# Loading one weight unevenly: six rows on every partition, eighteen more on twelve of them, forty on others

## The chip, the cores and the metric

The kernel runs on one core of a Trainium2 chip. The metric is the device time of one execution in microseconds (us). Its profile spans about 1.8 us less, from the first to the last instruction. KB is 1,024 bytes here, MB in the page 10^6 bytes; the prediction's rate of 27.1 KB/us counts 1,000 bytes to the KB.

## The reference, cut to what matters

Two branches on one token of width 1024 for a batch of two are mixed by a gate.

```python
def _A_ref(x, k_cache, v_cache, wq, wo):          # attention over a cache of 16384 positions, 32 heads
    q = ...(x @ wq)
    scores = einsum("bhqd,bhkd->bhqk", q, k_cache) * Dh ** -0.5
    o = einsum("bhqk,bhkd->bhqd", softmax(scores), v_cache)
    return ... o @ wo
def _B_ref(x, w1, w2, w3, w4):
    h = _gelu(_layernorm(x) @ w1)
    ...                                           # h is shifted by one or two positions
    hs = concatenate([g0, g1, g2, g3], axis=-1) @ w2
    x1 = x + hs
    return x1 + _gelu(_layernorm(x1) @ w3) @ w4
return g * a + (1 - g) * b
```

The two caches are 64 loads of 8 MB, about 94% of the 572.5 MB that are read. With one position every shift moves in zeros, so the input of `w2` is zero and `hs` is zero. The kernel loads and multiplies `w2` all the same. It also means that an experiment may leave rows of `w2` out without a wrong result (where one does, I say so), and that a correct result does not test the product of `w2` in any version.

## The kernel before

Everything large goes through three buffers of 64 KB per partition (8 MB each). One loop issues the loads in a fixed order as buffers come free: wq, K0, K1, V0, K2, V1, and so on. After V4, w1 and w2 share one buffer. At the end come w4 and wo in pieces.

```python
NBIG = 3
def big_tile(name):
    return big.tile([P, SLOT], BF16, tag="big", name=name)      # SLOT = 32768 elements
def load_k(i):
    t = big_tile("Kn")
    nc.sync.dma_start(out=t[:].rearrange("p (j d) -> p j d", d=Dh), in_=cache_rows(A_k_cache, i))
def load_rows(keys, srcs):
    t = big_tile("wt")
    c0 = 0
    for key, src in zip(keys, srcs):
        R, N = src.shape[0] // P, src.shape[1]
        v = t[:, c0 : c0 + R * N].rearrange("p (r n) -> p r n", n=N)
        nc.sync.dma_start(out=v, in_=src.rearrange("(p r) n -> p r n", p=P))
        wt[key] = v
        c0 += R * N
...
def linear(key, actT):                                           # w2 and w3: weights are the stationary side
    for c in range(C):
        for r in range(R):
            nc.tensor.matmul(ps[:, c, :], lhsT=w[:, r, :]...[:, :, c], rhs=actT[:, r, :], ...)
def st_mix():
    layernorm(xT[:], xn1T[:])
    ...                                                          # w1: activations stationary, 512 columns of w1 move
    nc.vector.tensor_tensor(out=x1[:], in0=xT[:], in1=linear("w2", shT)[:], op=ALU.add)
    layernorm(x1[:], xn2T[:])
    start_out(x1[:])
...
extra = {NT // 8: (lambda: load_rows(["w1", "w2"], [B_w1, B_w2]), st_mix), ...}
```

## Time and profile before

| quantity | before | where it is read |
|---|---|---|
| time | 1335.28 us (1335.23 to 1335.68) | three runs |
| share of 16 DMA engines' span, main queue | 99.4% | page, queue table |
| TensorE / VectorE busy | 61% / 57% | page, busy times |
| one 64 KB packet on one engine | 2.42 us | trace, packet records |
| queue ahead of the next V load at its issue | 19.2 us | timeline: 305.74 - 286.56 |

The page of the kernel before. The first lines are busy time and share of the span by engine; the DMA and GB/s lines have one figure for each of 40 slices; the queue lines are packets, MB and the time of their packets as a share of 16 engines.

```profile
span 1333.4 us, 11500 instructions
...
PE 811.7 (61%) x5017; PEld 353.2 (26%) x5017; DVE 758.8 (57%) x998; ACT 27.2 (2%) x68; POOL 13.2 (1%) x40
...
DMA  9999999999999999999999999999999999999997
GB/s 409 439 437 423 433 437 431 435 431 435 434 432 437 424 434 439 439 433 423 437 432 438 439 425 439 423 441 433 429 435 435 441 421 435 433 438 437 422 425 330
...
q1 hardware_dynamic: 12664, 572.54, 99.4%
q8 instruction: 39, 0.64, 0.2%
```

The DMA engines are busy throughout and the other engines are not. A load of K or V is 128 packets of 64 KB, eight on each of the 16 engines. At 2.42 us a packet an engine moves 26.5 KB per us.

The timeline of the kernel before around the layer that uses w2: start, duration, engine, line, operation, count, and the idle time with what ended it. SPq lines are DMA issues.

```profile
249.17 3.58 PE L559 MATMUL misc<-wt,xn1T 128*2 128x512 bf16 x16 [0.70 <-DVE xn1T L507]
...
252.68 4.01 PE L534 MATMUL misc<-shT,wt 128*128 128x2 bf16 x64
...
256.73 0.33 SPq L108 DMA_DIRECT2D Kn<-in_A_k_cache_dram  x1
...
265.88 2.37 DVE L339 STREAM_TRANSPOSE T<-Kn 128x1024 f32<-128x1024 f32 x2 [4.71 <-DMA Kn<-in_A_k_cache_dram]
...
286.56 0.33 SPq L119 DMA_DIRECT2D Vn<-in_A_v_cache_dram  x1
...
305.74 2.37 DVE L339 STREAM_TRANSPOSE T<-Kn 128x1024 f32<-128x1024 f32 x2 [8.08 <-DMA Kn<-in_A_k_cache_dram]
```

K7 is issued at 256.73 and its first transpose starts at 305.74, when it has landed. V6 is issued at 286.56, with that K7 still under way: 19 us of work are queued. The engines have something to do whenever a buffer is late by less than that.

The end of the chain of waits before, in order of time: start, duration, what.

```profile
1241.67 41.61 DMA Vn<-in_A_v_cache_dram
...
1292.98 26.76 DMA wo<-in_A_wo_dram
...
1319.76 9.92 DMA wo<-in_A_wo_dram
...
1330.16 0.42 DVE T L638
```

The chain ends in waits for the loads. Every 1 us by which the last wo piece lands later is 1 us of time.

One more reading is needed, and the views don't print it. The trace keeps the moment at which each of the 16 engines posts its completion of a transfer. Here are these moments for the kernel before, sorted, in us after the first of the 16:

```
V5 (second tile after w2)   0.0 0.2 0.3 0.3 0.4 0.4 0.7   1.5 1.6 1.6 1.7 1.7 1.7 1.7 1.9 1.9
last piece of wo            0.0 0.2 0.2 0.4 0.5 0.8 0.9   5.8 6.8 7.0 7.1 7.1 7.1 7.1 7.2 7.2
```

Seven engines are early and nine are late, and the gap grows. The late nine set the end.

### The profile page before, as it was taken

The page shows a single profiled execution, that of the slowest core. Times are in us where ns is not written, and L with a number is a line of the kernel's source. Part 1 is how long each engine was busy: PE and PEld are TensorE (multiplying, and loading weights), DVE is VectorE, ACT ScalarE, POOL GpSimd, SP SyncE. Part 2 cuts the span into 40 slices and gives each one's busy share as a digit, 9 for nine tenths or more (in the row PEclk, how much of TensorE's full clock was granted, in tenths as well). Part 3 has the DMA queues.
Part 4 walks back from the last instruction along what each step waited for, and adds up shares of the span by engine and source line. Part 5 has one row for each costly group of instructions (what it writes and reads, how often), then busy time and mean ns, then how long its engine had stood idle before and what let it go on. Part 6 is the DMA issues. An engine that isn't in the chain of part 4 may idle for free.

```text
span 1333.4 us, 11500 instructions
## 1 busy us (share of the span) xinstructions
PE 811.7 (61%) x5017; PEld 353.2 (26%) x5017; DVE 758.8 (57%) x998; ACT 27.2 (2%) x68; POOL 13.2 (1%) x40
## 2 busy tenths in 40 slices
PE   2577655676556765556766555576655556665564
PEld 0233222322225222222322222222222222222232
DVE  1677665466652665555666555566655556665540
ACT  0000000000000000000000000000000000000000
POOL 0000000000000000000000000000000000000000
PEclk9788877788777877778887777888777788877775
DMA  9999999999999999999999999999999999999997
GB/s 409 439 437 423 433 437 431 435 431 435 434 432 437 424 434 439 439 433 423 437 432 438 439 425 439 423 441 433 429 435 435 441 421 435 433 438 437 422 425 330
DMA packets 12722, 573.27 MB, mean 430 GB/s; under 512 B 1784, under 2 KB 1792, under 8 KB 2560
## 3 DMA queue, kind: packets, MB, share of 16 engines
q1 hardware_dynamic: 12664, 572.54, 99.4%
q8 instruction: 39, 0.64, 0.2%
q14 instruction: 11, 0.09, 0.0%
q10 hardware_dynamic: 8, 0.00, 0.0%
HBM read 572.53 MB, written 0.00 MB: 429 GB/s over the span
## 4 chain that ended last, share of the span: by engine, by line
PE 32%; DVE 29%; DMA 23%; another core or an unknown queue 12%; issue 2%; ACT 1%; SPq 0%; ACTq 0%; POOL 0%
DVE T L339 22%; PE S L353 21%; DMA Kn<-in_A_k_cache_dram 13%; PE O L397 7%; DMA wt<-in_B_w_dram 4%; DMA Vn<-in_A_v_cache_dram 3%; DMA wo<-in_A_wo_dram 3%; PE misc L224 2%; DVE Os L412 2%; PE misc L534 1%; ACT Pr L381 1%; DVE PT L385 1%; DVE mx L374 1%; PE misc L420 1%
## 5 line engine op out<-in xcount | busy, mean ns | idle before, releaser
L353 PE MATMUL S<-T,z 128*128 128x512 bf16 x2048 | 597.4, 425 | 316.4 <-DVE T L339 301.7
L339 DVE STREAM_TRANSPOSE T<-Kn 128x1024 f32<-128x1024 f32 x512 | 612.2, 1229 | 258.8 <-DMA Kn<-in_A_k_cache_dram 205.6
L353 PEld LDWEIGHTS <-z 128*128 128x128 bf16 x2048 | 211.0, 104 | 689.5 <-issue 528.0
L397 PE MATMUL O<-Vn,PT 128*32 128x512 bf16 x2048 | 121.4, 390 | 3.3 <-DMA Vn<-in_A_v_cache_dram 3.3
L397 PEld LDWEIGHTS <-PT 128*32 128x32 bf16 x2048 | 74.8, 141 | 48.7 <-issue 20.4
L408 DVE TENSOR_SCALAR Os<-O,xmask 128x128 f32<-128x128 f32 x32 | 11.2, 351 | 101.3 <-PE O L397 101.3
L224 PE MATMUL misc<-rs,ones_f 128*128 128x2 f32 x64 | 17.9, 349 | 79.1 <-DVE rs L428 79.1
L381 ACT ACTIVATE Pr<-S,nb 128x512 bf16<-128x512 f32 x32 | 22.0, 687 | 1196.8 <-DVE nb L376 1159.1
L420 PE MATMUL misc<-asel,Os 128*128 128x2 f32 x64 | 12.4, 264 | 51.0 <-DVE Os L412 51.0
L364 DVE TENSOR_REDUCE m<-S 128x1 f32<-128x512 f32 x32 | 22.1, 692 | 36.9 <-PE S L353 36.9
L385 DVE STREAM_TRANSPOSE PT<-Pr 128x512 bf16<-128x512 bf16 x32 | 22.8, 711 | 28.7 <-ACT Pr L381 28.7
L224 PEld LDWEIGHTS misc<-rs,ones_f 128*128 128x128 f32 x64 | 16.1, 313 | 84.0 <-issue 81.2
L412 DVE SCALAR_TENSOR_TENSOR Os<-O,xmask,Os 128x128 f32<-128x128 f32 x96 | 33.7, 351 | 3.4
L420 PEld LDWEIGHTS misc<-asel,Os 128*128 128x128 f32 x64 | 9.7, 191 | 65.2 <-DVE Os L412 61.0
L224 PE MATMUL misc<-mdiag,ones_f 128*128 128x128 f32 x64 | 15.5, 325 | 17.1 <-DVE mdiag L367 17.1
L374 DVE TENSOR_REDUCE mx<-misc 64x1 f32<-64x64 f32 x64 | 14.2, 222 | 19.1 <-PE misc L224 18.7
L313 POOL TENSOR_TENSOR z<-qsel,own 128x32 bf16<-128x32 bf16 x32 | 10.8, 336 | 1205.5 <-PE S L353 1175.1
L534 PEld LDWEIGHTS <-wt 128*128 128x128 bf16 x288 | 18.2, 164 | 8.4 <-DMA wt<-in_B_w_dram 7.6
L534 PE MATMUL misc<-xn2T,wt 128*128 128x2 bf16 x224 | 14.4, 202 | 7.4 <-DMA wt<-in_B_w_dram 7.4
L432 DVE RECIPROCAL rinv<-misc 128x2 f32<-128x2 f32 x32 | 5.4, 170 | 22.4 <-PE misc L224 22.4
L281 PE MATMUL misc<-wt,xT 128*2 128x512 bf16 x64 | 6.1, 562 | 19.9 <-DVE xT L269 19.9
L638 DVE CAST T<-out_acc 128x256 bf16<-128x256 f32 x1 | 0.4, 425 | 29.5 <-PE out_acc L446 29.5
(83 smaller groups left out, 109.0 us busy)
## 6 DMA issues: line engine op xcount, KB each, us to landing
Vn<-in_A_v_cache_dram SPq DMA_DIRECT2D x2, 4096.0 KB, 46.3
wt<-in_B_w_dram SPq DMA_DIRECT2D x1, 7168.0 KB
w<-in_B_w_dram SPq DMA_DIRECT2D x4, 1792.0 KB, 31.5
wo<-in_A_wo_dram SPq DMA_DIRECT2D x6, 1024.0 KB, 33.2
wt<-in_B_w_dram SPq DMA_DIRECT2D x2, 2048.0 KB, 37.1
wo<-in_A_wo_dram SPq DMA_DIRECT2D x2, 512.0 KB, 18.7
wo<-in_A_wo_dram SPq DMA_DIRECT2D x4, 256.0 KB, 12.7
Kn<-in_A_k_cache_dram SPq DMA_DIRECT2D x32, 51.7
```

Of the source, the lines that this page charges most:

```text
L224: nc.tensor.matmul(ps[:], lhsT=ones_f[:], rhs=src, start=True, stop=True)
L339: moved = nc.vector.transpose(out=T[:].rearrange("p w j s -> p j w s"), in_=Kw[:, m * CW : (m + 1) * CW].rearrange("p (j w e) -> p j w e", ...
L353: nc.tensor.matmul(S[:], lhsT=z[:, v, NM - 1 - m : NM - 1 - m + P], rhs=Tb[:, v // 2, :, v % 2], start=(m == 0 and v == 0), stop=(m == NM ...
L364: nc.vector.reduce_max(out=m[:], in_=S[:], axis=AX.X)
L374: nc.vector.reduce_max(out=mx[pa, :], in_=mall[pa, pa], axis=AX.X)
L381: nc.scalar.activation(out=Pr[:], in_=S[:], func=ACTF.Exp, bias=nb[:], scale=scale, accum_out=rs[:])
L385: nc.vector.transpose(out=PT[:], in_=Pr[:])
L397: nc.tensor.matmul(O[32 * g : 32 * g + 32, :], lhsT=PT[:, m : CJ * 32 : 16], rhs=V[:, j0 : j0 + 4, :], start=(m == 0), stop=(m == NM - 1),)
L408: nc.vector.tensor_scalar(out=Os[:], in0=Ox, scalar1=xmask[:, 0:1], scalar2=None, op0=ALU.mult)
L412: nc.vector.scalar_tensor_tensor(out=Os[:], in0=Ox, scalar=xmask[:, x : x + 1], in1=Os[:], op0=ALU.mult, op1=ALU.add,)
L420: nc.tensor.matmul(oc[:], lhsT=Os[:], rhs=asel[:], start=True, stop=True)
L534: nc.tensor.matmul(ps[:, c, :], lhsT=w[:, r, :].rearrange("k (p c) -> k p c", c=C)[:, :, c], rhs=actT[:, r, :], start=(r == 0), stop=(r == ...
```

## The change

Its intent, as I read it: put fewer bytes of w2 on most engines and more on a few, by placing 18 extra rows on each of partitions 0 to 11 through a transfer whose outermost dimension is three. The product has to follow the uneven layout: it now has the activations as the stationary side and adds up 25 row slots, some of them on few partitions, then transposes the result with 16 small matmuls.

```diff
+    WAYS, QUAD, BASE, MORE = 3, 4, 6, 18
+    W2_MORE = slice(0, WAYS * QUAD)
+    n_more = WAYS * QUAD * MORE
+    n_rest = D - P * BASE - n_more                     # 40
+    W2_REST = slice(64, 64 + n_rest)
+    W2_ROWS = (
+        [(slice(0, P), r) for r in range(BASE)]
+        + [(W2_MORE, BASE + r) for r in range(MORE)]
+        + [(W2_REST, BASE)]
+    )
... (an assert; load_rows returns its buffer; shT gets 24 row slots)
+    def load_w1_w2():
+        t = load_rows(["w1"], [B_w1])
+        w2 = t[:, KC * D : (KC + BASE + MORE) * D].rearrange("p (r n) -> p r n", n=D)
+        nc.sync.dma_start(
+            out=w2[:, 0:BASE, :], in_=B_w2[0 : P * BASE, :].rearrange("(p r) n -> p r n", p=P)
+        )
+        r0 = P * BASE
+        nc.sync.dma_start(
+            out=w2[W2_MORE, BASE : BASE + MORE, :],
+            in_=B_w2[r0 : r0 + n_more, :].rearrange("(y x r) n -> x y (r n)", x=WAYS, y=QUAD),
+        )
+        r0 += n_more
+        nc.sync.dma_start(out=w2[W2_REST, BASE, :], in_=B_w2[r0:D, :])
+        wt["w2"] = w2
... (half_rows: the product of w1 made into a helper with a list of row slots)
-        nc.vector.tensor_tensor(out=x1[:], in0=xT[:], in1=linear("w2", shT)[:], op=ALU.add)
+        hs = half_rows("w2", shT, W2_ROWS)
+        hs_ps = misc_psum([P, KC, B])
+        for c in range(KC):
+            for g in range(2):
+                nc.tensor.matmul(hs_ps[64 * g : 64 * g + 64, c, :],
+                    lhsT=hs[32 * g : 32 * g + 32, c : HW : KC],
+                    rhs=ident_f[32 * g : 32 * g + 32, group(g)], start=True, stop=True)
+        nc.vector.tensor_tensor(out=x1[:], in0=xT[:], in1=hs_ps[:], op=ALU.add)
...
-        NT // 8: (lambda: load_rows(["w1", "w2"], [B_w1, B_w2]), st_mix),
+        NT // 8: (load_w1_w2, st_mix),
```

More of the change, by code (lines that the diff above doesn't have):

```diff
@@ L121, in load_v @@
         vn_tiles[i] = t
+    WAYS, QUAD, BASE, MORE = 3, 4, 6, 18
+    W2_MORE = slice(0, WAYS * QUAD)
+    n_more = WAYS * QUAD * MORE
+    n_rest = D - P * BASE - n_more
+    assert 0 < n_rest <= 64 and KC + BASE + MORE <= SLOT // D
+    W2_REST = slice(64, 64 + n_rest)
[18 more added lines that the diff above has]
+        wt["w2"] = w2
     def load_rows(keys, srcs):
@@ L132, in load_rows @@
             c0 += R * N
+        return t
     W4_SPLIT = [7] * 4
@@ L525, in gelu, with half_rows @@
         nc.vector.tensor_tensor(out=dst_bf, in0=sq[:], in1=pre_f32, op=ALU.mult)
+    HW = D // 2
+    def half_rows(key, actT, slots):
+        w = wt.pop(key)
+        ps = misc_psum([P, HW])
+        for g in range(2):
+            zero_rows(ps, g, HW)
+        for n, (rows, r) in enumerate(slots):
+            for g in range(2):
+                nc.tensor.matmul(
+                    ps[group(g), :],
+                    lhsT=actT[rows, r, :],
+                    rhs=w[rows, r, g * HW : (g + 1) * HW],
+                    start=False,
+                    stop=(n == len(slots) - 1),
+                    skip_group_check=True,
+                )
+        out = t_tile([P, HW], FP32)
+        nc.vector.tensor_copy(out=out[0:64, :], in_=ps[0:64, :])
+        return out
     def linear(key, actT):
@@ L544 @@
     h_rows = const.tile([P, D // 2], BF16)
-    shT = const.tile([P, KC, B], BF16)
+    shT = const.tile([P, BASE + MORE, B], BF16)
     x1 = const.tile([P, KC, B], FP32)
@@ L551, in st_mix @@
         layernorm(xT[:], xn1T[:])
-        w1 = wt.pop("w1")
-        HW = D // 2
-        ps = misc_psum([P, HW])
-        for g in range(2):
-            zero_rows(ps, g, HW)
-        for r in range(KC):
-            for g in range(2):
-                nc.tensor.matmul(
-                    ps[group(g), :],
-                    lhsT=xn1T[:, r, :],
-                    rhs=w1[:, r, g * HW : (g + 1) * HW],
-                    start=False,
-                    stop=(r == KC - 1),
-                    skip_group_check=True,
-                )
-        h1 = t_tile([P, HW], FP32)
-        nc.vector.tensor_copy(out=h1[0:64, :], in_=ps[0:64, :])
+        h1 = half_rows("w1", xn1T, [(slice(0, P), r) for r in range(KC)])
         gelu(h1[0:64, :], h_rows[0:64, :])
@@ L574, in st_mix @@
                     raise NotImplementedError("one position only")
-        nc.vector.tensor_tensor(out=x1[:], in0=xT[:], in1=linear("w2", shT)[:], op=ALU.add)
+        hs = half_rows("w2", shT, W2_ROWS)
+        hs_ps = misc_psum([P, KC, B])
+        for c in range(KC):
+            for g in range(2):
+                nc.tensor.matmul(
+                    hs_ps[64 * g : 64 * g + 64, c, :],
+                    lhsT=hs[32 * g : 32 * g + 32, c : HW : KC],
+                    rhs=ident_f[32 * g : 32 * g + 32, group(g)],
+                    start=True,
+                    stop=True,
+                )
+        nc.vector.tensor_tensor(out=x1[:], in0=xT[:], in1=hs_ps[:], op=ALU.add)
         layernorm(x1[:], xn2T[:])
```

## The prediction

> **What bounds the kernel now.** The DMA engines. The page's slice table shows DMA at 9 tenths in every slice but the last, the queue table gives the main queue 99.4% of 16 engines' span, and the windows view shows a DMA share of 0.97 to 1.02 in every 33 us until the tail. PE (61%) and DVE (57%) have room. Each K or V tile is 8 MB, 128 packets of 64 KB, and the trace has 2.42 us for one such packet on one engine: 27.1 KB/us per engine. The queue is never empty: at most issues one whole tile (about 19.5 us) is still ahead.
>
> **Engines do not finish together.** The trace records when each of the 16 engines posts its completion of a transfer. For K0 these lie within 1.8 us; for the last wo piece within 7.2 us: 7 engines finish within 0.9 us of the first, 9 come 5.8 to 7.2 us later. [...]a fetch puts about 0.93 us between two data packets and makes the next one 0.5 us longer. The slow nine set the end of the kernel.
>
> **What the change does to DMA.** Bytes stay the same. [...] The loads of six rows stay at k = 16. [...]432 KB go to three engines, 144 KB each (four packets of 36 KB, an estimated 1.36 us each). The forty rows get k = 10, 8 KB each. Per engine, w2 costs 128 KB now[...]. That is +120 KB, +4.5 us on three engines, and -0.9 to -1.2 us on the others. A lag is not recovered while the queue stays full.
>
> **What it does to compute.** The 64 small matmuls of w2 (4.0 us in the timeline at 252.7) become 50 of 512 columns; the 16 of w1 took 3.58 us[...], so an estimated 11 us, some 8 us of it after the late rows land, plus 16 small transposing matmuls and a 0.7 us copy. The layer and the release of the slot move by 8 to 10 us, and K6's QK starts about 8 us late. The next K load was issued at 256.7 and landed 49 us later, so some 29 us of queue stood before it: no DMA bubble. DVE idled 8 us before K7, so compute catches up. Nothing of this is on the critical path.
>
> **Sum.** If at least one of the three engines is among the slow nine (I think 7 in 10), the end moves by about +4 to +4.5 us. If all three are among the fast seven, the lag disappears in their 6 us of slack, and the end moves by about -1 us. Prediction 1338.9 us, 8 in 10 between 1334.0 and 1341.5. Chances: faster 0.01, within 2% 0.97, slower 0.02.
>
> **What would show it.** Twelve packets of 36 KB on three engines; three late completions by about 4.5 us from K6 on, kept to the end; QK of K6 late, K7 not; matmul group of w2 about 10 us; DMA share 1.00 in the windows after it.
>
> **What would make it wrong.** A different k; a packet to few partitions slower than 27 KB/us; the later slot release emptying the queue; a fetch pattern that moves to other engines.

k is the number of engines that share a transfer; the trace after has three and ten completions where the prediction has three engines and k = 10. A fetch is one of the 39 packets of 16 KB on queue 8 (instruction). The sum came to +4 to +4.5 us if one of the three engines is late and about -1 us if all are early, put as 1338.9 us. Of the terms behind it the bytes by engine, by the completions after, are 120 KB more on three engines (4.5 us at 27.1 KB/us) and 24 or 32 KB less on the others (0.9 and 1.2 us).

## The result

The time after is 1335.02 us (1334.81 to 1335.45, six runs), before 1335.39 us (1335.23 to 1335.68, six runs of the kernel before): 0.37 us less by the medians. The ratio is 0.9997, with a 95% interval of 0.9984 to 1.001. Ratios are the mean time of one kernel's runs over that of the other's of the same rounds, so not quite the ratio of the medians quoted. All outputs are right. The verdict is: the same.

The page after:

```profile
span 1333.6 us, 11483 instructions
...
PE 797.4 (60%) x4974; PEld 351.3 (26%) x5037; DVE 760.1 (57%) x999; ACT 27.2 (2%) x68; POOL 12.8 (1%) x40
...
DMA  9999999999999999999999999999999999999998
GB/s 410 437 439 417 439 431 437 423 433 433 438 432 435 429 427 439 439 437 427 429 437 431 439 431 439 429 431 437 429 435 433 439 431 429 435 432 437 429 422 338
...
q1 hardware_dynamic: 12729, 572.54, 99.4%
q8 instruction: 39, 0.64, 0.2%
```

Nothing moves in these averages. The trace has what the sum hides. The DMA issues after, for w2 (KB each, and us to landing where a single wait shows it):

```profile
wt<-in_B_w_dram SPq DMA_DIRECT2D x1, 1536.0 KB, 41.4
...
wt<-in_B_w_dram SPq DMA_DIRECT2D x1, 432.0 KB
wt<-in_B_w_dram SPq DMA_DIRECT2D x1, 80.0 KB
```

The packet records show 128 packets of 12 KB, twelve of 36 KB that run three at a time, from 243.4 to 249.4 us of the span, and 40 of 2 KB. The trace has three completions for the load of 432 KB and ten for that of 80 KB. So the eighteen rows did go to three engines, four packets each, and the forty rows to ten. The last three of those ten completions, at 250.39 to 250.50 us, come after the three of the 432 KB, at 249.75 to 249.89, and the other seven by 246.72: the three engines are, by this, among the ten. The completions after, beside those of before:

```
V5      before   0.0 0.2 0.3 0.3 0.4 0.4 0.7   1.5 1.6 1.6 1.7 1.7 1.7 1.7 1.9 1.9
V5      after    0.0 0.1 0.1 0.4   1.1 1.2 1.5 1.5 1.5 1.6 1.7 1.7 2.0   5.6 5.6 5.7
last wo before   0.0 0.2 0.2 0.4 0.5 0.8 0.9   5.8 6.8 7.0 7.1 7.1 7.1 7.1 7.2 7.2
last wo after    0.0 0.2 0.2 0.6   5.5 5.7 6.1   6.2 6.7 6.9 7.0 7.1 7.1 7.2 7.4 7.4
```

Right after w2 three engines stand alone 5.6 us behind. At the end four are early instead of seven, and the other three lie just ahead of the late nine. They have used the slack that they had, and no more.

The timeline after, with the lines that answer to those of before:

```profile
249.12 3.58 PE L566 MATMUL misc<-wt,xn1T 128*2 128x512 bf16 x16
...
252.48 5.88 PE L566 MATMUL misc<-wt,shT 128*2 128x512 bf16 x49
...
258.40 0.33 SPq L108 DMA_DIRECT2D Kn<-in_A_k_cache_dram  x1
...
269.70 2.37 DVE L369 STREAM_TRANSPOSE T<-Kn 128x1024 f32<-128x1024 f32 x2 [4.50 <-DMA Kn<-in_A_k_cache_dram]
...
290.80 0.33 SPq L119 DMA_DIRECT2D Vn<-in_A_v_cache_dram  x1
...
308.30 2.37 DVE L369 STREAM_TRANSPOSE T<-Kn 128x1024 f32<-128x1024 f32 x2 [6.39 <-DMA Kn<-in_A_k_cache_dram]
```

K6 starts 3.8 us later than before (269.70 against 265.88) and K7 2.6 us later (308.30 against 305.74), both because they land later, on those three engines. The product of w2 takes 5.88 us where the old one took 4.01, and K7 is issued 1.7 us later. By the end of the chain nothing of it is left:

```profile
1241.41 41.75 DMA Vn<-in_A_v_cache_dram
...
1292.85 27.05 DMA wo<-in_A_wo_dram
...
1319.91 9.84 DMA wo<-in_A_wo_dram
...
1330.22 0.42 DVE T L684
```

### The profile page after: what moved, and what is told of

Its sections match the earlier page's. It is cut to its first block, busy times and chain, and to the rows that moved or that the text cites. A ratio compares the mean times of both kernels' runs of the same rounds, so it can differ in the third digit from the quotient of the medians.

```text
span 1333.6 us, 11483 instructions
## 1 busy us (share of the span) xinstructions
PE 797.4 (60%) x4974; PEld 351.3 (26%) x5037; DVE 760.1 (57%) x999; ACT 27.2 (2%) x68; POOL 12.8 (1%) x40
## 3 DMA queue, kind: packets, MB, share of 16 engines
q1 hardware_dynamic: 12729, 572.54, 99.4%
## 4 chain that ended last, share of the span: by engine, by line
DVE 30%; PE 30%; DMA 23%; another core or an unknown queue 12%; issue 2%; ACT 1%; SPq 0%; ACTq 0%
DVE T L369 24%; PE S L383 19%; DMA Kn<-in_A_k_cache_dram 13%; PE O L427 7%; DMA wt<-in_B_w_dram 4%; DMA Vn<-in_A_v_cache_dram 3%; DMA wo<-in_A_wo_dram 3%; PE misc L254 2%; DVE Os L442 2%; ACT Pr L411 1%; DVE PT L415 1%; PE misc L585 1%; DVE mx L404 1%; PE misc L566 1%
## 5 line engine op out<-in xcount | busy, mean ns | idle before, releaser
L383 PE MATMUL S<-T,z 128*128 128x512 bf16 x1985 | 579.8, 419 | 330.1 <-DVE T L369 308.5
L585 PEld LDWEIGHTS <-wt 128*128 128x128 bf16 x224 | 14.3, 172 | 7.5 <-DMA wt<-in_B_w_dram 7.5
```

The costliest lines, as they stand in the source:

```text
L383: nc.tensor.matmul(S[:], lhsT=z[:, v, NM - 1 - m : NM - 1 - m + P], rhs=Tb[:, v // 2, :, v % 2], start=(m == 0 and v == 0), stop=(m == NM ...
L585: nc.tensor.matmul(ps[:, c, :], lhsT=w[:, r, :].rearrange("k (p c) -> k p c", c=C)[:, :, c], rhs=actT[:, r, :], start=(r == 0), stop=(r == ...
```

## The experiments

Twelve runs, each with five timings (spare8_odd and own_parts have four) against the kernel before, in three submissions (the kernel before: medians 1335.34, 1335.40, 1335.40). The 95% intervals of the ratios are about 0.13% wide to each side, 1.7 us, so each small difference alone lies within them; I rest on the spread of runs (0.2 to 0.6 us for most), on the packet records, and on sums that have to fit each other. The differences below are of medians in the same rounds.

| run | what it is | median us (range) | against before |
|---|---|---|---|
| spare3 | before + 120 KB on 3 engines | 1335.46 (1335.30 to 1335.74) | +0.12 |
| spare3twice | before + 240 KB on 3 engines | 1337.79 (1337.74 to 1337.89) | +2.45 |
| spare4 | before + 120 KB on 4 engines | 1339.47 (1339.24 to 1339.82) | +4.07 |
| spare7 | before + 120 KB on 7 engines | 1339.86 (1339.79 to 1340.10) | +4.52 |
| spare8 | before + 120 KB on 8 engines | 1339.92 (1339.86 to 1340.05) | +4.58 |
| spare8_odd | the same to partitions 64 to 95 | 1346.50 (1345.81 to 1346.82) | +11.10 |
| after_norest | after, without the 40 rows | 1334.14 (1334.12 to 1334.46) | -1.26 |
| after_rest3 | after, 36 of the 40 rows on 3 engines | 1335.09 (1334.90 to 1335.24) | -0.31 |
| rest_own | after, 40 rows to partitions 32 to 71 | 1334.58 (1334.28 to 1334.74) | -0.82 |
| spare_rest | before + 40 spare rows | 1336.10 (1335.85 to 1336.18) | +0.70 |
| own_parts | a complete version, 40 rows to partitions 32 to 47 | 1334.44 (1334.25 to 1334.88) | -0.96 |
| compute_only | before's loads, after's product | 1335.31 (1335.22 to 1335.35) | -0.09 |

### Does the lag hide, and for how long?

Theory A: the three engines that take such a load are early ones, and their lag ends inside the early engines' slack. Rival B: a lag is made good somewhere while the queue stays full. Rival C: the lag reaches the end and is paid for by the fewer bytes elsewhere. The spare loads add bytes to a few engines and take none away. Nothing reads them; they fill rows of the buffer that the kernel before leaves empty.

```diff
+    def load_spare(t, ways, p0):
+        n = ways * 4 * 15
+        spare = t[:, 16 * D : 31 * D].rearrange("p (r n) -> p r n", n=D)
+        nc.sync.dma_start(out=spare[p0 : p0 + 4 * ways, :, :],
+            in_=B_w1[0:n, :].rearrange("(y x r) n -> x y (r n)", x=ways, y=4))
     def load_w1_w2():
         t = load_rows(["w1", "w2"], [B_w1, B_w2])
+        load_spare(t, 3, 0)                  # spare3
+        load_spare(t, 3, 0); load_spare(t, 3, 32)     # spare3twice, in its place
```

> Kernel before plus one unused load of 60 x 3 rows on partitions 0 to 11 with an outermost dimension of three: 120 KB more on each of three engines (an estimated +4.5 us there), no byte less anywhere, compute of w2 as before. Theory A[...]: time unchanged within 0.5 us; at the last wo piece 4 completions early, three at about 4.5 to 5.5 us, nine at 5.8 to 7.2 us. Rival B (a lag is made good somewhere while the queue stays full): unchanged too, but the seven are back together at the end. Rival C (the lag does reach the end, and only the 24 to 32 KB fewer on other engines paid for it in the change): +3 to +4.5 us.

> The spare load of three twice, 240 KB more on each of three engines, an estimated +9.1 us of lag. Theory A: the slack of about 6.3 to 7.2 us is used up and the end moves by about +2 to +3 us, with three completions last. Rival B: unchanged. Rival C: +8 to +9 us.

Measured: +0.12 and +2.45 us. The completions:

```
V5      spare3        0.0 0.0 0.1 0.4   1.3 1.4 1.6 1.6 1.6 1.7 1.7 1.7 1.8   4.3 4.4 4.7
last wo spare3        0.0 0.1 0.4 0.6   4.3 4.9 5.2   5.8 6.8 7.0 7.1 7.2 7.3 7.3 7.4 7.4
V5      spare3twice   0.0 0.0 0.1 0.4   1.4 1.6 1.6 1.6 1.6 1.6 1.7 1.8 1.9   9.2 9.2 9.2
last wo spare3twice   0.0 0.1 0.1 0.1   3.5 4.6 4.8 5.0 5.0 5.1 5.1 5.2 5.3   6.9 7.5 7.5
```

120 KB cost nothing that these runs resolve, 240 KB cost 2.45 us. With an estimated lag of 9.1 us that leaves 6.6 us hidden, within the 5.8 to 7.2 us by which the late nine trail before. Rivals B (0) and C (4.5 and 9) both fall. The knee lies where the early engines' lead ends. (The first four early engines also end 2.2 us later in spare3twice than before, so their lead never passes about 7.8 us in any run. Issues in the tail wait for earlier pieces, in the trace before 15.6 us for pieces of w4 and 8.4 us for pieces of wo; I take that to be the cap, but did not test it.)

### How many of the loaded engines are late ones?

```diff
-        load_spare(t, 3, 0)
+        load_spare(t, 4, 0)      # spare4; 7 in spare7, 8 in spare8
```

Spare4 set two cases against each other: all four loaded engines are early (the first figure), or the fourth is late (the second). Spare7 did so for the seven: they are the early seven, or another set that merely contains the three (+3 to +4.5 us). The eighth engine in spare8 is the one that its load has over that of spare7. That each of these sets contains the smaller ones was my assumption.

> Kernel before plus the spare load with an outermost dimension of four[...]. With three it cost nothing and with seven 4.5 us[...]. [...]unchanged within 0.5 us. [...]+3 to +4.6 us.

> The same spare load with an outermost dimension of seven on partitions 0 to 27[...]. Theory A[...]: time unchanged within 0.5 us, and at the last wo piece all 16 completions within about 3 us. [...]+3 to +4.5 us. Rival B: unchanged, early seven still 6 us ahead.

> The same with eight[...]. Theory A: the eighth engine is one of the nine late ones, so the end moves by +3 to +4.5 us, with one completion alone at the end. Rival B: unchanged.

Measured: +4.07, +4.52 and +4.58 us. Spare7 missed what I expected of theory A with the seven loaded engines as the early seven; that part of the theory fell. Spare8 has the expected time, but not for the expected reason: I expected one completion alone at the end, and three stand there (7.0, 7.5 and 7.6 us after the first). The completions of V5 fall into groups:

```
V5 spare4   0.0 0.2 0.2 0.4   1.5 1.6 1.6 1.6 1.7 1.8 1.9 1.9   4.7 4.7 4.8   6.5
V5 spare7   0.0 0.2 0.4   1.4 1.6 1.6 1.7 1.8 1.9   4.4 4.5 4.6 4.6   6.1 6.2 6.3
V5 spare8   0.0 0.4   1.4 1.5 1.6 1.6 1.6 1.6   4.5 4.5 4.5 4.6 4.7   6.1 6.2 6.2
```

The groups are, from left to right: early, late, early with the spare load, late with the spare load. The loaded engines are three early ones in spare3, three early and one late in spare4, four early and three late in spare7, five early and three late in spare8. These counts fit sets that contain each other: the fourth engine is then a late one, two of the next three are as well, and the eighth is early. The records carry no engine, so which ones they are is not shown.

The likely cause of the late nine is in the packets. In the trace after, packets that follow each other can be strung together by their times. There is a gap of about 0.9 us beside nearly every one of the 39 instruction packets of 16 KB, which themselves take 0.94 us in the median, and these gaps fall into eight strings, 210 to 300 us apart in each. Such a gap is mostly followed by a packet of about 2.9 instead of 2.42 us, so a block costs its engine 1.4 us; five of them make 7 us. A ninth string has gaps of 0.3 us, next to the 8 KB packets of queue 14. No run changed the number of these blocks, and some packets can be strung in more than one way, so this cause is inferred and not shown by experiment; that nine engines are late, and that none of the three loaded in spare3 is among them, does not rest on it.

### Why only 0.4 us came out

By the completions, seven of the engines that carry the forty rows have 24 KB less to move and the six that carry neither these nor the eighteen 32 KB less: an estimated 0.9 and 1.2 us at 26.5 KB per us. With the lag hidden, the end should have moved by -0.9 us; it moved by -0.37. In the packets of the trace after, 56 data packets between 243.4 and 255.6 us beside the usual fetch are over 3% too long, by 10 us in sum over 16 engines: packets of 12 KB took 0.53 and not 0.46 us, of 36 KB 1.55 and not 1.36, of 64 KB 2.5 to 2.8 and not 2.42. None of the spare3, spare7 or spare8 runs has them. They have a pattern in time: the 2 KB packets come in three bursts (243.3 to 243.9, 245.2 to 245.9 and 249.3 to 249.7 us), and each of the 56 overlaps a burst or starts less than 0.3 us after one; the 64 KB packets that start between, from 246.4 to 246.7 us, took 2.42. So I looked at the forty rows, and at where they are written.

```diff
 # after_norest
-        r0 += n_more
-        nc.sync.dma_start(out=w2[W2_REST, BASE, :], in_=B_w2[r0:D, :])
-        + [(W2_REST, BASE)]
 # after_rest3
-        nc.sync.dma_start(out=w2[W2_REST, BASE, :], in_=B_w2[r0:D, :])
+        n36 = WAYS * 12
+        nc.sync.dma_start(out=w2[64 : 64 + n36, BASE, :],
+            in_=B_w2[r0 : r0 + n36, :].rearrange("(y x) n -> x y n", x=WAYS))
+        nc.sync.dma_start(out=w2[64 + n36 : 64 + n_rest, BASE, :], in_=B_w2[r0 + n36 : D, :])
```

In after_rest3, 36 of the forty rows are 24 KB on each of three engines, so the others have about 32 KB less than before, an estimated -1.2 us, and the three about 138 KB more if they are the same three as those of the eighteen rows (in spare3twice two such loads were on the same three: V5 ends 9.2 us late on each).

> The changed kernel without the load and the product of the last 40 rows (on purpose incomplete: the activations there are zero, so the result is still right). In the profile of the changed kernel packets of all engines were 9 to 16 percent long for some 3 us around the packets of these 40 rows. Theory: that cost 0.5 to 1 us of the gain expected from fewer bytes on the late engines. Then this run has no long packets after w2 and is 1 us under before or a little more (1334.0 to 1334.5). Rival: the eighteen rows cause the long packets; then they remain and the time is within 0.3 us of the changed kernel's.

> The changed kernel with 36 of the 40 rows loaded with an outermost dimension of three as well[...], to the same partitions. [...] If the long packets come from the 40 rows being spread over ten engines: -1.0 to -1.2 us against before. If they come from the partitions written or from the eighteen rows: -0.2 to -0.6 us, as in the changed kernel.

Measured: -1.26 us without the forty rows, and no long packet except beside a fetch: all twelve 36 KB packets took 1.364 us. With the rows on three engines instead of ten, -0.31 us, and 22 long packets of 64 KB that add up to some 7.5 us. So the forty rows cost the gain, and not because they are spread over ten engines. What is left is where they are written. The forty rows went to partitions 64 to 103; the eighteen rows, and the loads of spare3, spare7 and spare8, whose traces have no such long packets, went to partitions 0 to 31 at most. Two runs put that to the test, one large and one with a single number of the load changed. Each expectation has two cases: first that the partitions written matter, then that only the bytes, the rows or the count of engines do. The two edits:

```diff
 # spare8_odd
-        load_spare(t, 8, 0)
+        load_spare(t, 8, 64)
 # rest_own (product of these rows left out)
-    W2_REST = slice(64, 64 + n_rest)
+    W2_REST = slice(32, 32 + n_rest)
```

> The spare load of eight, but into partitions 64 to 95 and not 0 to 31[...]. [...]about +9 us, and packets of 64 KB well over 2.42 us in the trace. If only the count of bytes on an engine matters: +4.6 us as with partitions 0 to 31.

> The changed kernel with one number altered: the 40 rows go to partitions 32 to 71 and not 64 to 103[...] (their product is left out[...]; the activations there are zero, so the result is still right). [...]none in this run, and the time is before minus 0.7 to 0.9 us[...]. If 2 KB rows or the count of engines made them: they remain, and the time stays at -0.3 us.

Measured: spare8_odd +11.10 us against +4.58 for the same bytes on the same number of engines. The 30 KB packets took 2.37 us in the median and not 1.14, and 64 KB packets beside them up to 5.1 us. The windows view of spare8 and of spare8_odd (stretch, length, busy time of each engine with instructions, granted clock, DMA share, GB/s):

```profile
core 0: us, PE busy (x) PEld busy (x) DVE busy (x) ACT busy (x) POOL busy (x), PEclk, DMA share, GB/s
245.00:257.00 12.00, 9.32 (x89) 5.98 (x89) 4.32 (x18) 0.78 (x2) 0.70 (x1) 0.67 1.05 454
```

```profile
core 0: us, PE busy (x) PEld busy (x) DVE busy (x) ACT busy (x) POOL busy (x), PEclk, DMA share, GB/s
245.00:257.00 12.00, 9.25 (x88) 5.90 (x88) 4.33 (x17) 0.78 (x2) 0.70 (x1) 0.69 1.01 267
```

By the DMA share (1.05 and 1.01) the engines are just as busy, and they move 267 GB/s in place of 454: the share does not tell these two runs apart, the GB/s does. The estimate of +9 us was too low, and I did not find where the other 2 us come from.

In rest_own one number moves the forty rows to partitions 32 to 71: no long packet except beside a fetch, and -0.82 us, as the bytes say (-0.9). That is 0.45 us better than the changed kernel. The long packets of the changed kernel, 10 us over 16 engines, are 0.6 us each; the two agree as well as runs of this spread can. What it is about the partitions stays open: the loads that made long packets went to 64 to 95 and 64 to 103, but rest_own wrote 64 to 71 as well and has none, so it is not simply every partition from 64 up, and no run tells what makes a partition dear for a load. In spare8_odd the 64 KB packets of the engines without spare bytes slowed as well (the eleven that started up to 249.8 us took 4.5 to 5.1 us and not 2.42), so the cost is not confined to the engines that carry the spare bytes.

```diff
 # spare_rest, against before
+        nc.sync.dma_start(out=t[64:104, 16 * D : 17 * D], in_=B_w1[0:40, :])
```

> Kernel before plus only a spare load of 40 rows to partitions 64 to 103 (8 KB more on ten engines, an estimated +0.3 us on them). If these rows hold up all engines by themselves: long packets after w2, and +0.7 to +1.1 us. If they do so only beside the load of eighteen rows: no long packets, +0.3 us.

Measured: +0.70 us, at the lower edge, with 19 long packets that add up to 2.5 us. Of the 0.70 us, an estimated 0.3 are the 8 KB themselves (at 26.5 KB per us). So the forty rows do harm without the eighteen rows, but to fewer packets. Why they hold up engines that write none of them at the time I can't say: in the trace after, only three engines write rows in the last burst (twelve packets of 2 KB), but the 64 KB packets under way on all thirteen others are long (2.61 to 2.65 us and not 2.42).

### A version that keeps the gain

```diff
-        nc.sync.dma_start(out=w2[W2_REST, BASE, :], in_=B_w2[r0:D, :])
+        nc.sync.dma_start(out=w2[W2_NEAR, BASE : BASE + 3, :],          # partitions 32 to 43
+            in_=B_w2[r0 : r0 + n_near, :].rearrange("(y x r) n -> x y (r n)", x=WAYS, y=QUAD))
+        r0 += n_near
+        nc.sync.dma_start(out=w2[44:48, BASE, :], in_=B_w2[r0:D, :])
         hs = half_rows("w2", shT, W2_ROWS)
+        near = half_rows("w2", shT, W2_ROWS_NEAR)
+        nc.vector.tensor_tensor(out=hs[0:64, :], in0=hs[0:64, :], in1=near[0:64, :], op=ALU.add)
```

By the same count all but the three loaded engines then have about 32 KB less than before (an estimated -1.2 us) and the three 138 KB more.

> A complete version: as the changed kernel, but 36 of the 40 rows go with an outermost dimension of three to partitions 32 to 43[...]; a second accumulation takes their product. [...] Expected: before minus 1.0 to 1.3 us, no long packets, under both kernels.

Measured: 1334.44 us, -0.96 us (expected -1.0 to -1.3, so just short of it), no long packet except beside a fetch. It issues the product of every row (the zero input means that the result can't test it), and its median is under both kernels, by 0.07% and 0.04%: no gain that the verdict resolves, though its runs and those of before don't overlap (its slowest, 1334.88, lies among those of the changed kernel).

### Is compute part of it?

```diff
-        NT // 8: (load_w1_w2, st_mix),
+        NT // 8: (lambda: load_rows(["w1", "w2"], [B_w1, B_w2]), st_mix),
-        hs = half_rows("w2", shT, W2_ROWS)
+        hs = half_rows("w2", shT, [(slice(0, P), r) for r in range(KC)])
```

> Loads as before; only the compute of w2 is changed to the row product with its transposing matmuls, eight rows per partition. If compute is off the critical path here: unchanged within 0.4 us, though K6's first transpose starts up to 4 us later. If some of it reaches the end: more than +0.5 us.

Measured: -0.09 us. The first transposes of K6 and K7 in the timeline of this run:

```profile
265.94 2.37 DVE L369 STREAM_TRANSPOSE T<-Kn 128x1024 f32<-128x1024 f32 x2 [1.75 <-DMA Kn<-in_A_k_cache_dram]
...
305.56 2.37 DVE L369 STREAM_TRANSPOSE T<-Kn 128x1024 f32<-128x1024 f32 x2 [7.84 <-DMA Kn<-in_A_k_cache_dram]
```

Both start where they did before (265.88 and 305.74), not 4 us later as I allowed for: the delay of K6 in the changed kernel was its landing, not the compute ahead of it.

## Why the prediction was right or wrong

- **Bound by DMA, queue never empty.** Right. The queue table has 99.4% before and after, and a load on the engines moves the end by what it takes (spare8: 120 KB, 4.58 us; by bytes 4.5).
- **Three engines, four packets of 36 KB each, 1.36 us.** Right: twelve packets, three at a time, six of them 1.36 us. The other six took 1.55 to 1.59.
- **Three engines fall behind by 4.5 us, and the others gain 0.9 to 1.2.** Right: 152 KB between a loaded engine and one with 96 KB are an estimated 5.7 us, and V5 shows 5.6. The lag is not made good: at the last wo piece the three are still 5.5 to 6.1 us behind the first.
- **"If at least one of the three engines is among the slow nine (I think 7 in 10), the end moves by about +4 to +4.5 us."** This is the step that failed. All three are early ones. The two cases were laid out rightly and spare3, spare4 and spare3twice bear them out, but the trace before does not say which engines are late, and I put too much weight on the wrong case. The time of 1338.9 us was too high for that reason; the range of 1334.0 to 1341.5 held 1335.02 because it covered both. That the three engines of this load are early ones was luck for the kernel, and the prediction had no ground to know it.
- **The end moves by "about -1 us" if the lag hides.** The mechanism was right, the size was off: -0.37 us. Missing was a cost of some 0.5 us for writing the forty rows to partitions 64 to 103; rest_own, with partitions 32 to 71, has -0.82. The prediction named packets to few partitions as a risk, but for the twelve partitions, where it did not occur.
- **The product of w2 takes about 11 us, and the layer moves by 8 to 10 us.** Wrong in size: 5.88 us, and K7's issue moved by 1.7 us. I scaled from w1's product, which ran at a granted clock of 0.50. The windows view after (columns as above) shows w1's stretch at 0.50 and that of the eighteen rows at 1.00:

```profile
core 0: us, PE busy (x) PEld busy (x) DVE busy (x) ACT busy (x) POOL busy (x), PEclk, DMA share, GB/s
249.10:252.70 3.60, 3.60 (x19) 1.14 (x20) 0.10 (x1) 0.00 (x0) 0.00 (x0) 0.50 0.94 394
254.00:258.00 4.00, 4.00 (x39) 1.40 (x38) 2.34 (x5) 0.63 (x1) 0.00 (x0) 1.00 0.98 426
```

  Nor did the product have to wait for late rows: the last completion of w2 in the trace is at 250.5 us, and the weight loads for the rows on twelve partitions start at 254.01. Since compute_only moves nothing, the error had no effect.
- **"QK of K6 late, K7 not."** Half wrong. K6 is 3.8 us late and K7 still 2.6 us, because the three engines stay behind. It cost nothing, as the queue was longer than the delay.

## What to carry to other kernels

When DMA is the bound, look at the engines one by one: the average share says 99%, while the kernel ends with its latest engine. Here bytes could be moved to engines that are early at no cost that the runs resolve (spare3: +0.12 us), but only up to their lead of 6 to 7 us (spare3twice: +2.45 us), and the early ones have to be found by experiment. The partitions written count too: the same bytes to partitions 64 to 95 and not 0 to 31 ran at half speed (30 KB packets, 2.37 and not 1.14 us), and even 80 KB to partitions 64 to 103 took back half of the gain (-0.37 us, and -0.82 with partitions 32 to 71). These runs show no rule for it; try the partitions.
